# A fused linear-attention and feed-forward kernel: the feed-forward's hidden units renumbered, its first weight loaded by row chunks

## The chip, the cores and the metric

The kernel runs on one core of a Trainium2 chip. The metric is the device time of one execution in microseconds (us); the numbers given are medians of repeated runs. A core has five engines that run their own instruction streams: TensorE (PE; its weight loads are listed apart as PEld), VectorE (DVE), ScalarE (ACT), GpSimd (POOL) and SyncE (SP), which here issues the DMA transfers. An engine waits for another by a counting semaphore: GpSimd, for example, raises its count by one with each finished instruction, and a reader waits until the count stands at a given number.

## The reference

Inputs are q, k, v of 8 batches, 8 heads, 576 positions and 64 features in float32, and two weights: w_in (512 x 2048) and w_out (2048 x 512).

```python
def phi(x, c, s):
    r = np.maximum(x, 0.0)
    return np.concatenate([r * c, r * s], axis=-1)
q_p = phi(q, cos_w, sin_w)
k_p = phi(k, cos_w, sin_w)
kv = np.einsum('bhsf,bhsd->bhfd', k_p, v)
z = np.sum(k_p, axis=2)
num = np.einsum('bhsf,bhfd->bhsd', q_p, kv)
den = np.einsum('bhsf,bhf->bhs', q_p, z)[..., None] + 1e-06
attn_out = num / den
# tokens x 512, heads side by side
x = attn_out.transpose(0, 2, 1, 3).reshape(B * S, H * D)
h = x @ w_in
g = np.maximum(0.01 * h, h)
return g @ w_out
```

The order of the 2048 hidden units is free: the sum over them in the last product is the same if w_in's columns and w_out's rows are numbered in the same way.

## The kernel before

All matrix work is in fp16 with float32 sums. A batch's first 512 positions form one group of four tiles of 128 tokens (`MAIN`), and the last 64 positions of all eight batches form a ninth group, so the feed-forward runs over nine groups of 512 tokens (`g` = 0 to 8). For a group:

- `q_prep` (line 287) makes phi(q) on VectorE, `q_transpose` (312) turns it on PE through PSUM, and ScalarE copies it out. `k_main`, `k_tail`, `v_main`, `v_tail` (229 to 247) make phi(k) and v in fp16.
- `kv_half` (277) sums kv and z for four heads on PE and copies the sum out on ScalarE. `num` (321) multiplies one tile of queries by kv for all heads; `num_half` (353) does it for two tiles (a pair `jp`) and four heads (`hg`). `divide` (335) is three VectorE instructions behind either.
- `x_transpose` (386) turns one tile of attention output, `x_transpose_half` (368) a pair of tiles for four heads; ScalarE copies the result into `xT`, whose four row chunks of 128 are the 512 inputs of the feed-forward.
- `ffn1(g, m, lo, hi, chunks)` (396) computes one unit: 128 hidden units for token columns `lo` to `hi`, as one matmul for each row chunk, with a piece of `w1` as PE's weights. Two units share a PSUM tile `ps_h` of two banks, and one ScalarE Lrelu (412) takes the pair into `g`.
- `ffn2(g, i)` (416) computes one of four parts of a tile's output from four units of `g` and of `w2`; `ffn2_out` writes it.

The weights arrive in float32 in staging tiles and are cast to fp16 into `w1` and `w2`, both resident. The staging pool (`stage`, seven buffers, line 56) is shared with q, k and v. `load_w1` (128) loads columns `W1[i]` to `W1[i+1]` of w_in for all four row chunks: four pieces of 256 columns and two of 512. `load_w2` (134) loads 512 rows of w_out as four blocks of 128 rows, so that a partition takes four rows of 2 KB from four places. All loads go through SP's one queue.

The order of the instructions on each engine is that of the program text (`tc.manual_schedule()`); the framework adds the waits, from the regions that each instruction reads and writes. In the first batch (lines 480 to 529) the text is written out by hand: attention and ffn1 of group 0 are interleaved, ffn1 works on the first two tiles (`half` = 256 columns) as soon as these are there, then on the other two. `cast_w1` 0, 1 and 2 on GpSimd are recorded ahead of the first ffn1, 3 on VectorE further down (520), 4 and 5 after unit 7 (531 to 533). `idle(n)` issues n matmuls on a blank tile. From line 545 `weave` mixes units and steps by position numbers: group 0's remaining units, group 0's ffn2 with batch 1's attention, and then all other groups, in which ffn1 of the next group alternates with ffn2 of this one.

Of the kernel before, what the change touches and what calls it, by code (L numbers as in the profile page):

```python
# [9 lines left out]
dt = mybir.dt  # L10
AF = mybir.ActivationFunctionType
ALU = mybir.AluOpType

P = 128
J = 4
# [3 lines left out]
def kernel(  # L19
# [14 lines left out]
    nc = tc.nc  # L34
# [3 lines left out]
    DFF = moe_w_in.shape[1]  # L38
    MAIN = J * P
# [3 lines left out]
    NKC = DM // P  # L43
    NFT = DFF // P
# [5 lines left out]
    def pool(name, bufs, space=None):  # L50
        kw = {"space": space} if space is not None else {}
        return ctx.enter_context(tc.tile_pool(name=name, bufs=bufs, **kw))
# [3 lines left out]
    stage = pool("stage", 7)  # L56
# [11 lines left out]
    ps_h = pool("ps_h", 2, PS)  # L68
# [3 lines left out]
    def psum(where, shape, dtype, name):  # L72
        p = {"h": ps_h, "o": ps_o, "n": ps_n}[where]
        return p.tile(shape, dtype, name=name, tag="ps_" + where)

    st = {}
    ACT, DVE, POOL = nc.scalar, nc.vector, nc.gpsimd
# [42 lines left out]

    w1 = const.tile([P, NKC, DFF], dt.float16, name="w1")
    w2 = const.tile([P, NFT, DM], dt.float16, name="w2")

    W1 = [0, 256, 512, 768, 1024, 1536, 2048]
    w1v = moe_w_in.rearrange("(c p) f -> p c f", p=P)
    w2v = moe_w_out.rearrange("(m p) d -> p m d", p=P)

    def load_w1(i):
        lo, hi = W1[i], W1[i + 1]
        t = stage.tile([P, NKC, hi - lo], dt.float32, name="w1st", tag="stage")  # L130
        nc.sync.dma_start(t, w1v[:, :, lo:hi])
        st["w1", i] = t

    def load_w2(i):
        t = stage.tile([P, 4, DM], dt.float32, name="w2st", tag="stage")
        nc.sync.dma_start(t, w2v[:, 4 * i : 4 * i + 4, :])
        st["w2", i] = t

    load_main("q", q, 0, (0,))
# [1 line left out]
    load_kvtail("k", k, 0)  # L141
    load_kvtail("v", v, 0)
    load_halves(0)
    for i in range(4):
        load_w1(i)

# [3 lines left out]
    def idle(n):  # L152
        ps = psum("o", [P, MAIN], dt.float32, "ps_idle")
        for _ in range(n):
            nc.tensor.matmul(ps, lhsT=blank[:, 0:P], rhs=blank)  # L155
# [40 lines left out]
    for i in range(2):  # L196
# [5 lines left out]
        for o in range(2):  # L202
            sl = slice(o * TAIL, (o + 1) * TAIL)
# [15 lines left out]
    def copy(eng, o, i):  # L219
        if eng is ACT:  # L220
            nc.scalar.copy(o, i)  # L221
        else:
            eng.tensor_copy(o, i)  # L223
# [5 lines left out]
    def k_main(b, j, eng_c, eng_s, lo=0, hi=H):  # L229
        kpm, kst = st["kpm", b], st["k", b]  # L230
        for eng, t, f in ((eng_c, cos_t, 0), (eng_s, sin_t, D)):
            phi_half(
                eng, kpm[:, lo:hi, j, f : f + D], kst[:, lo:hi, j, :], t[:, j : j + 1]
            )
# [6 lines left out]
    def v_main(b, lo, hi, eng):  # L241
        copy(eng, vmain[b % 2][:, lo:hi, :, 0:D], st["v", b][:, lo:hi])
# [78 lines left out]
    def num(g, j, where="n"):  # L321
        qpT = st["qpT", g, j]
        ps = psum(where, [P, 2, 512], dt.float32, "ps_num")
        for b, lo, hi in q_src(g, j)[2]:
            for h in range(H):
                nc.tensor.matmul(  # L326
                    ps[lo:hi, h // 4, (h % 4) * NE : (h % 4 + 1) * NE],
                    lhsT=qpT[:, h, lo:hi],
                    rhs=kv[b][:, h, :],
                )  # L330
        xs = xspool.tile([P, H, D], dt.float16, name="xs")
        divide(ps, xs.rearrange("p (a b) e -> p a b e", a=2))
        st["xs", g, j] = xs
# [19 lines left out]
    def num_half(g, jp, hg, where):  # L353

        if hg == 0:
            st["xp", g, jp] = qppool.tile([P, 2, H, D], dt.float16, name="xp", tag="qp")
        ps = psum(where, [P, 2, 512], dt.float32, "ps_numh")
        for o in range(2):
            for hh in range(4):
                h = 4 * hg + hh  # L360
                nc.tensor.matmul(  # L361
                    ps[:, o, hh * NE : (hh + 1) * NE],
                    lhsT=st["qpT", g, 2 * jp + o][:, h, :],
                    rhs=kv[g][:, h, :],
                )
        divide(ps, st["xp", g, jp][:, :, 4 * hg : 4 * hg + 4, :])

    def x_transpose_half(g, jp, hg, ps=None, out=True):

        if ("xT", g) not in st:  # L370
            st["xT", g] = xtpool.tile([P, NKC, MAIN], dt.float16, name="xT")
        xp = st["xp", g, jp]
        if ps is None:
            ps = psum("o", [P, 2, 2 * P], dt.float16, "ps_xth")
        for cc in range(2):
            for o in range(2):
                h = 4 * hg + 2 * cc
                nc.tensor.transpose(
                    ps[:, cc, o * P : (o + 1) * P], xp[:, o, h : h + 2, :], ident
                )  # L380
        if out:
            nc.scalar.copy(  # L382
                st["xT", g][:, 2 * hg : 2 * hg + 2, jp * 2 * P : (jp + 1) * 2 * P], ps
            )

    def x_transpose(g, j, where="o"):
        xs = st["xs", g, j]
        ps = psum(where, [P, NKC, P], dt.float16, "ps_xt")
        for c in range(NKC):
            nc.tensor.transpose(ps[:, c, :], xs[:, 2 * c : 2 * c + 2, :], ident)  # L390
        nc.scalar.copy(xT_tile(g, j), ps)  # L391

    def ffn1(g, m, lo=0, hi=MAIN, chunks=range(NKC)):

        if ("g", g) not in st:
            st["g", g] = gpool.tile([P, NFT, MAIN], dt.float16, name="g")
        if m % 2 == 0 and chunks[0] == 0:
            st["h", m // 2] = psum("h", [P, 2, MAIN], dt.float32, "ps_h")  # L400
        xT = st["xT", g]
        ps = st["h", m // 2]
        for c in chunks:
            nc.tensor.matmul(  # L404
                ps[:, m % 2, lo:hi],
                lhsT=w1[:, c, m * P : (m + 1) * P],
                rhs=xT[:, c, lo:hi],
                start=(c == 0),
                stop=(c == NKC - 1),
            )  # L410
        if m % 2 == 1 and chunks[-1] == NKC - 1:
            nc.scalar.activation(  # L412
                st["g", g][:, m - 1 : m + 1, lo:hi], ps[:, :, lo:hi], AF.Lrelu
            )

    def ffn2(g, i, eng=DVE):
        tt, part = divmod(i, 4)
# [51 lines left out]
            queue = ACT if half and o else nc.sync  # L469
            queue.dma_start(out[r0 : r0 + TAIL, cols], osb[o * TAIL : (o + 1) * TAIL, :])  # L470

    def cast_w1(i, eng):
        copy(eng, w1[:, :, W1[i] : W1[i + 1]], st["w1", i])

    def cast_w2(i, eng):
        copy(eng, w2[:, 4 * i : 4 * i + 4, :], st["w2", i])
# [14 lines left out]
    for j in range(J):  # L491
        k_main(0, j, DVE, DVE, 0, 4)
    v_main(0, 0, 4, ACT)
    idle(6)
    kv_half(0, 0, "o")
    for j in range(J):
        k_main(0, j, ACT if j < 2 else DVE, DVE, 4, 8)
    v_main(0, 4, 6, DVE)
    v_main(0, 6, 8, ACT)
    idle(1)  # L500
    num_half(0, 0, 0, "n")
    idle(4)
    kv_half(0, 1, "o")
    for i in range(3):
        cast_w1(i, POOL)
    x_transpose_half(0, 0, 0)
    num_half(0, 0, 1, "h")
    num(0, 2, "n")
    half = 2 * P
    for m in range(2):  # L510
        ffn1(0, m, 0, half, range(0, 2))
    idle(1)
    x_transpose_half(0, 0, 1)
    for m in range(2, 4):
        ffn1(0, m, 0, half, range(0, 2))
    for m in range(2):
        ffn1(0, m, 0, half, range(2, 4))
    x_transpose(0, 2)
    num(0, 3, "n")
    cast_w1(3, DVE)  # L520
    for m in range(2, 4):
        ffn1(0, m, 0, half, range(2, 4))
    for m in range(4, 6):
        ffn1(0, m, 0, half)
    x_transpose(0, 3)
    for m in range(6, 8):
        ffn1(0, m, 0, half)
    for m in range(8):
        ffn1(0, m, half, MAIN)

    for i in range(4, 6):
        load_w1(i)
        cast_w1(i, POOL)
    load_w2(0)
    load_main("q", q, 1)
    load_kvtail("k", k, 1)
    load_kvtail("v", v, 1)
    for i in range(1, 4):
        load_w2(i)
    load_halves(1)  # L540
    load_main("q", q, 2)
# [3 lines left out]
    def weave(units, steps):  # L545

        steps = sorted(steps, key=lambda s: s[0])
        for at, u in units:
            while steps and steps[0][0] <= at:
                steps.pop(0)[1]()  # L550
            u()
        assert not steps

    def f1(g, m):
        return lambda: ffn1(g, m)
# [4 lines left out]
    steps = []  # L560

    def at(pos, f, *args):
        steps.append((pos, lambda: f(*args)))

    at(12, cast_w2, 0, DVE)
    weave([(m, f1(0, m)) for m in range(8, NFT)], steps)

    for j in range(J):  # L570
        q_prep(1, j)
    cast_w2(1, DVE)
    cast_w2(2, DVE)
    kp_tiles(1)
    k_tail(1, DVE, DVE)
# [2 lines left out]
    ps = psum("n", [P, 2, DM], dt.float32, "ps_o")  # L578
    for tt in range(2):
        st["ps_o", 0, 2 + tt] = ps[:, tt]  # L580
    steps = []
    for j in range(J):
        at(2 + j, q_transpose, 1, j, ACT, "h")
        at(9, k_main, 1, j, ACT, DVE, 0, 4)
    at(9, v_main, 1, 0, 2, DVE)
    at(9, v_main, 1, 2, 4, ACT)
# [19 lines left out]
    ps = psum("n", [P, 2, MAIN], dt.float16, "ps_x")  # L606
# [29 lines left out]
    steps = []  # L636
# [84 lines left out]
```

## Time and profile before

| What | Value |
|---|---|
| Median of 3 runs | 297.73 us (297.64 to 298.7) |
| The profiled execution | 297.93 us, of which the profiled span is 295.9 us |
| Instructions | 4849 |
| DMA | 56.93 MB, 91301 packets |
| L404 (ffn1) on PE | 608 matmuls, 143.0 us |
| L425 (ffn2) on PE | 560 matmuls, 139.3 us |
| L404 weight loads (PEld) | 608, mean 98 ns |
| L412 Lrelu on ACT | 76, mean 979 ns |
| L223 casts of w_in on POOL | 5, mean 1381 ns |

A row of the profile names a line of the kernel, the engine, the operation and the tiles (out <- in). In an order of time the first number is the start in us from the span's beginning, the second the time until the last of the merged instructions has ended; x is their number; the brackets tell how long the engine was idle before and what ended the wait. Matmuls overlap, so the mean time of one (368 ns for L404) is longer than the step from one to the next.

### The profile page before, as it was taken

The page shows a single profiled execution, that of the slowest core. Times are in us where ns is not written, and L with a number is a line of the kernel's source. Part 1 is how long each engine was busy: PE and PEld are TensorE (multiplying, and loading weights), DVE is VectorE, ACT ScalarE, POOL GpSimd, SP SyncE. Part 2 cuts the span into 40 slices and gives each one's busy share as a digit, 9 for nine tenths or more (in the row PEclk, how much of TensorE's full clock was granted, in tenths as well). Part 3 has the DMA queues.
Part 4 walks back from the last instruction along what each step waited for, and adds up shares of the span by engine and source line. Part 5 has one row for each costly group of instructions (what it writes and reads, how often), then busy time and mean ns, then how long its engine had stood idle before and what let it go on. Part 6 is the DMA issues. An engine that isn't in the chain of part 4 may idle for free.

```text
span 295.9 us, 4849 instructions
## 1 busy us (share of the span) xinstructions
PE 287.2 (97%) x1950; PEld 146.9 (50%) x1950; DVE 133.4 (45%) x329; ACT 108.2 (37%) x132; POOL 22.0 (7%) x33
## 2 busy tenths in 40 slices
PE   7889999999999999999999999999999999999994
PEld 3567556455455454454445444544444444444444
DVE  5950668934754927723861356233323211000011
ACT  4855546665163422242223222322222232222200
POOL 2045000000000400200400040000000000000000
PEclk9999999999999999999999999999999999999999
DMA  7999999999999999989659985716671211011132
GB/s 215 348 366 372 322 366 347 325 154 325 258 257 290 203 293 264 226 196 302 178 124 230 315 148 125 110 53 144 139 162 55 71 53 38 35 47 60 38 71 71
DMA packets 91301, 56.93 MB, mean 192 GB/s; under 512 B 56848, under 2 KB 83728, under 8 KB 91280
## 3 DMA queue, kind: packets, MB, share of 16 engines
q1 hardware_dynamic: 91200, 56.57, 74.1%
q8 instruction: 15, 0.25, 0.4%
q10 hardware_dynamic: 80, 0.07, 0.1%
q14 instruction: 6, 0.05, 0.0%
HBM read 36.70 MB, written 9.44 MB: 156 GB/s over the span
## 4 chain that ended last, share of the span: by engine, by line
PE 81%; DMA 11%; ACT 3%; SPq 2%; DVE 1%; issue 0%; POOL 0%
PE ps_h L404 37%; PE ps_o L425 36%; DMA qst<-in_q_dram 7%; DMA vst<-in_v_dram 3%; PE ps_num L326 3%; SPq L86 2%; PE ps_kv L263 2%; ACT qpT L221 1%; DMA out_dram<-osb 1%; PE ps_kvh L263 1%; ACT xT L382 1%; PE ps_kv L253 0%; PE ps_numh L361 0%; ACT g L412 0%; ACT xT L609 0%
## 5 line engine op out<-in xcount | busy, mean ns | idle before, releaser
L404 PE MATMUL ps_h<-xT,w 128*128 128x512 f16 (+1 forms) x608 | 143.0, 368 | 1.4 <-ACT xT L391 0.8
L425 PE MATMUL ps_o<-w,g 128*128 128x512 f16 x560 | 139.3, 379 | 0.0
L412 ACT ACTIVATE g<-ps_h 128x1024 f16<-128x1024 f32 (+1 forms) x76 | 74.3, 979 | 143.3 <-PE ps_h L404 143.2
L404 PEld LDWEIGHTS <-w 128*128 128x128 f16 x608 | 57.0, 98 | 60.0 <-issue 1.6
L425 PEld LDWEIGHTS <-g 128*128 128x128 f16 x560 | 54.1, 98 | 63.0
L223 DVE COPY osb<-ps_o 128x512 f32<-128x512 f32 x33 | 22.7, 691 | 81.1 <-PE ps_o L425 80.9
L337 DVE TENSOR_SCALAR den<-ps_num 128x8 f32<-128x8 f32 x30 | 5.0, 166 | 53.9 <-PE ps_num L326 53.9
L342 DVE TENSOR_TENSOR xs<-ps_num,rden 128x512 f16<-128x512 f32 x30 | 20.7, 691 | 1.0
L223 POOL CAST vmain<-vst 128x1024 f16<-128x1024 f32 (+1 forms) x9 | 9.7, 1096 | 134.4 <-DMA vst<-in_v_dram 86.3
L215 DVE TENSOR_SCALAR qp<-qst,cos_t 128x512 f16<-128x512 f32 (+1 forms) x34 | 16.6, 488 | 4.0 <-DMA qst<-in_q_dram 4.0
L215 DVE TENSOR_SCALAR kpm<-kst,sin_t 128x512 f16<-128x512 f32 (+1 forms) x40 | 18.0, 466 | 0.3 <-DMA kst<-in_k_dram 0.3
L215 DVE TENSOR_SCALAR qp<-qst,sin_t 128x512 f16<-128x512 f32 (+1 forms) x34 | 16.0, 469 | 0.0
L326 PEld LDWEIGHTS <-qpT 128*128 128x128 f16 (+1 forms) x272 | 11.9, 101 | 7.4 <-issue 1.7
L215 DVE TENSOR_SCALAR kpm<-kst,cos_t 128x512 f16<-128x512 f32 (+1 forms) x29 | 13.9, 480 | 0.1
L326 PE MATMUL ps_num<-kv,qpT 128*128 128x66 f16 (+1 forms) x272 | 13.3, 194 | 0.0
L263 PEld LDWEIGHTS <-kpm 128*128 128x128 f16 x256 | 10.6, 97 | 2.4 <-DVE kpm L215 0.7
L155 PE MATMUL ps_idle<-blank 128*128 128x512 f16 x30 | 9.7, 457 | 1.2 <-DVE blank L150 1.2
L221 ACT COPY qpT<-ps_qt 128x1024 f16<-128x1024 f16 x8 | 7.8, 1019 | 4.7 <-PE ps_qt L316 4.7
L223 DVE CAST w<-w2st 128x2048 f16<-128x2048 f32 x4 | 4.9, 1227 | 10.0 <-DMA w2st<-in_moe_w_out_dram 10.0
L223 POOL CAST w<-w1st 128x1024 f16<-128x1024 f32 (+1 forms) x5 | 6.9, 1381 | 19.1 <-DMA w1st<-in_moe_w_in_dram 19.1
L263 PE MATMUL ps_kv<-vmain,kpm 128*128 128x66 f16 x192 | 8.1, 193 | 0.0
L341 DVE RECIPROCAL rden<-den 128x8 f32<-128x8 f32 x36 | 7.3, 203 | 1.2
(58 smaller groups left out, 100.0 us busy)
## 6 DMA issues: line engine op xcount, KB each, us to landing
out_dram<-osb SPq DMA_DIRECT2D x32, 256.0 KB, 2.8
qst<-in_q_dram SPq DMA_DIRECT2D x7, 1024.0 KB, 6.6
kst<-in_k_dram SPq DMA_DIRECT2D x6, 1024.0 KB, 7.6
vst<-in_v_dram SPq DMA_DIRECT2D x6, 1024.0 KB, 7.9
w2st<-in_moe_w_out_dram SPq DMA_DIRECT2D x4, 1024.0 KB, 10.2
kst<-in_k_dram SPq DMA_DIRECT2D x4, 512.0 KB, 8.6
vst<-in_v_dram SPq DMA_DIRECT2D x4, 512.0 KB, 8.4
w1st<-in_moe_w_in_dram SPq DMA_DIRECT2D x4, 512.0 KB, 9.2
```

What stands on the lines that cost most here:

```text
L86: nc.sync.dma_start(st[nm, b][:, lo:hi], src[b, lo:hi, 0:MAIN, :].rearrange("h (p j) d -> p h j d", j=J),)
L155: nc.tensor.matmul(ps, lhsT=blank[:, 0:P], rhs=blank)
L215: eng.tensor_scalar(out=o, in0=i, scalar1=0.0, scalar2=col, op0=ALU.max, op1=ALU.mult)
L221: nc.scalar.copy(o, i)
L223: eng.tensor_copy(o, i)
L263: nc.tensor.matmul(ps[:, (2 * cc + o) * NE : (2 * cc + o + 1) * NE], lhsT=kpm[:, h, j, :], rhs=vmain[b % 2][:, h, j, :], start=False, stop ...
L326: nc.tensor.matmul(ps[lo:hi, h // 4, (h % 4) * NE : (h % 4 + 1) * NE], lhsT=qpT[:, h, lo:hi], rhs=kv[b][:, h, :],)
L341: nc.vector.reciprocal(rden, den)
L342: nc.vector.tensor_tensor(out=xs, in0=ps[:, :, 0 : 4 * NE].rearrange("p a (b e) -> p a b e", e=NE)[:, :, :, 0:D], in1=rden.rearrange("p (a ...
L404: nc.tensor.matmul(ps[:, m % 2, lo:hi], lhsT=w1[:, c, m * P : (m + 1) * P], rhs=xT[:, c, lo:hi], start=(c == 0), stop=(c == NKC - 1),)
L412: nc.scalar.activation(st["g", g][:, m - 1 : m + 1, lo:hi], ps[:, :, lo:hi], AF.Lrelu)
L425: nc.tensor.matmul(ps, lhsT=st["g", g][:, m, tt * P : (tt + 1) * P], rhs=w2[:, m, :], start=(m == 0), stop=(m == NFT - 1),)
```

## The change

The hidden units get a new numbering. In block i (512 units) unit 4i + r now holds w_in's columns 512i + 4p + r for p = 0 to 127, and w_out's rows of the same numbers. A partition of `w2` thus takes four consecutive rows, 8 KB, and PE reads its ffn1 weights out of `w1` at every fourth column. w_in is loaded in eight pieces, (block, row-chunk pair), each of 128 partitions x 2 chunks x 512 columns, all issued at the start; eight casts on GpSimd, recorded ahead of the first ffn1, take their place. In the first batch both pairs of tiles now go through `num_half` and `x_transpose_half`; ffn1's units 0 to 3 run over both halves, chunks 0 and 1 first, then 2 and 3; units 4 to 15 run over 512 columns, the first two in the PSUM tile "n". Two of `k_main`'s calls move ahead of `kv_half(0, 0)`. w_out's second piece is loaded ahead of batch 1's q, its cast moves to position 14, and batch 1's four `q_transpose` move three positions back.

```diff
-    W1 = [0, 256, 512, 768, 1024, 1536, 2048]
+    NB = DFF // 512
     w1v = moe_w_in.rearrange("(c p) f -> p c f", p=P)
-    w2v = moe_w_out.rearrange("(m p) d -> p m d", p=P)
+    w1m = w1.rearrange("q c (i p r) -> q c i r p", p=P, r=4)
+    w2v = moe_w_out.rearrange("(i p r) d -> i p r d", p=P, r=4)
...
+    def load_w1(i, cp):
+        if cp == 0:
+            st["w1", i] = stage.tile([P, NKC, 512], dt.float32, name="w1st", tag="stage")
+        sl = slice(2 * cp, 2 * cp + 2)
+        nc.sync.dma_start(st["w1", i][:, sl], w1v[:, sl, 512 * i : 512 * (i + 1)])
...
-        nc.sync.dma_start(t, w2v[:, 4 * i : 4 * i + 4, :])
+        nc.sync.dma_start(t, w2v[i])
...
-    for i in range(4):
-        load_w1(i)
+    for i in range(NB):
+        for cp in range(2):
+            load_w1(i, cp)
...
-                lhsT=w1[:, c, m * P : (m + 1) * P],
+                lhsT=w1m[:, c, m // 4, m % 4, :],
                 rhs=xT[:, c, lo:hi],
-                start=(c == 0),
-                stop=(c == NKC - 1),
+                start=(c == 0 and lo == 0),
+                stop=(c == NKC - 1 and hi == MAIN),
...
-    def cast_w1(i, eng):
-        copy(eng, w1[:, :, W1[i] : W1[i + 1]], st["w1", i])
+    def cast_w1(i, cp, eng):
+        sl = slice(2 * cp, 2 * cp + 2)
+        copy(eng, w1[:, sl, 512 * i : 512 * (i + 1)], st["w1", i][:, sl])
...
+    for j in range(2):
+        k_main(0, j, ACT, DVE, 4, 8)
     idle(6)
     kv_half(0, 0, "o")
-    for j in range(J):
-        k_main(0, j, ACT if j < 2 else DVE, DVE, 4, 8)
+    for j in range(2, J):
+        k_main(0, j, DVE, DVE, 4, 8)
...
     num_half(0, 0, 0, "n")
-    idle(4)
+    num_half(0, 1, 0, "h")
+    idle(3)
     kv_half(0, 1, "o")
-    for i in range(3):
-        cast_w1(i, POOL)
+    for i in range(NB):
+        for cp in range(2):
+            cast_w1(i, cp, POOL)
     x_transpose_half(0, 0, 0)
-    num_half(0, 0, 1, "h")
-    num(0, 2, "n")
+    num_half(0, 0, 1, "n")
     half = 2 * P
     for m in range(2):
         ffn1(0, m, 0, half, range(0, 2))
-    idle(1)
-    x_transpose_half(0, 0, 1)
+    x_transpose_half(0, 1, 0)
     for m in range(2, 4):
         ffn1(0, m, 0, half, range(0, 2))
...
+    num_half(0, 1, 1, "n")
+    x_transpose_half(0, 0, 1)
+    for m in range(4):
+        ffn1(0, m, half, MAIN, range(0, 2))
+    x_transpose_half(0, 1, 1)
+    for m in range(4):
         ffn1(0, m, 0, half, range(2, 4))
...
+    for m in range(4):
+        ffn1(0, m, half, MAIN, range(2, 4))
...
-    for i in range(4, 6):
-        load_w1(i)
-        cast_w1(i, POOL)
-    load_w2(0)
+    for i in range(2):
+        load_w2(i)
...
+    for m in range(4, 6):
+        ffn1(0, m, where="n")
     at(12, cast_w2, 0, DVE)
-    weave([(m, f1(0, m)) for m in range(8, NFT)], steps)
+    at(14, cast_w2, 1, DVE)
+    weave([(m, f1(0, m)) for m in range(6, NFT)], steps)
```

## The prediction

> **What bounds the kernel now.** I read the table by stage first, then TensorE's (PE's) order of time, then who waited. The stage rows give, after the stretch, its length, busy time of PE, PEld, DVE, ACT, POOL, the granted clock, the DMA share and GB/s.
>
> ```profile
> PE 287.2 (97%) x1950; PEld 146.9 (50%) x1950; DVE 133.4 (45%) x329; ACT 108.2 (37%) x132; POOL 22.0 (7%) x33
> ...
> 15.50:22.20 6.70, 5.45 (x67) 4.01 (x66) 3.78 (x10) 4.17 (x8) 3.04 (x3) 1.00 1.08 368
> 22.20:33.50 11.30, 11.30 (x73) 7.07 (x74) 1.78 (x3) 6.06 (x8) 3.79 (x2) 1.00 1.09 341
> 33.50:62.00 28.50, 27.73 (x219) 15.03 (x218) 23.38 (x58) 18.22 (x27) 0.61 (x1) 1.00 1.12 330
> 62.00:284.00 222.00, 222.00 (x1440) 108.97 (x1438) 90.32 (x211) 69.75 (x75) 12.47 (x16) 1.00 0.68 161
> 292.20:295.30 3.10, 0.00 (x0) 0.00 (x0) 0.00 (x0) 0.33 (x1) 0.00 (x0) 1.00 0.28 71
> 295.40:295.80 0.40, 0.00 (x0) 0.00 (x0) 0.00 (x0) 0.00 (x0) 0.00 (x0) 0.50 0.00 0
> ```
>
> From 22.2 us on PE is busy in every microsecond but some 0.8, all of them before 62. Whatever delays PE in the first 35 us therefore reaches the end undiminished, and whatever brings it forward reaches the end only until the next input is late. The DMA engines are saturated to 62 us (330 to 368 GB/s). The last two rows matter below: PE's last matmul ends at 292.1, and the clock is 1.00 until 295.3, then 0.50.
>
> ```profile
> 1.19 5.16 PE L155 MATMUL ps_idle<-blank 128*128 128x512 f16 x14 [1.19 <-DVE blank L150]
> 15.43 1.04 POOL L223 CAST w<-w1st 128x1024 f16<-128x1024 f32 x1 [12.63 <-DMA w1st<-in_moe_w_in_dram]
> 16.55 0.60 PE L404 MATMUL ps_h<-xT,w 128*128 128x256 f16 x4
> 16.93 1.04 POOL L223 CAST w<-w1st 128x1024 f16<-128x1024 f32 x1 [0.47 <-DMA w1st<-in_moe_w_in_dram]
> 18.55 1.04 POOL L223 CAST w<-w1st 128x1024 f16<-128x1024 f32 x1 [0.58 <-DMA w1st<-in_moe_w_in_dram]
> 21.44 0.69 DVE L223 CAST w<-w1st 128x1024 f16<-128x1024 f32 x1 [0.51 <-DMA w1st<-in_moe_w_in_dram]
> 22.20 11.45 PE L404 MATMUL ps_h<-xT,w 128*128 128x256 f16 x72 [0.80 <-ACT xT L391]
> 24.18 1.89 POOL L223 CAST w<-w1st 128x2048 f16<-128x2048 f32 x1 [4.60 <-DMA w1st<-in_moe_w_in_dram]
> 26.89 1.89 POOL L223 CAST w<-w1st 128x2048 f16<-128x2048 f32 x1 [0.82 <-DMA w1st<-in_moe_w_in_dram]
> 33.48 1.89 PE L425 MATMUL ps_o<-w,g 128*128 128x512 f16 x8
> 48.98 0.57 PE L263 MATMUL ps_kvh<-vmain,kpm 128*128 128x66 f16 x8 [0.21 <-POOL vmain L223]
> ```
>
> Each cast starts as its piece of w_in lands. With 1 KB packets 0.5 MB takes 1.50 to 1.62 us (15.43, 16.93, 18.55); with 2 KB packets 1 MB takes 2.71 (24.18 to 26.89), so 1.36 per 0.5 MB. PE's paces: a 512-column matmul 216 ns (four in 0.86 in the chain of waits); a 256-column one 109 (the 72 of 22.20 end their issue at 33.48, 11.28 us later; less 32 x 0.216 leaves 4.37 for 40); a transpose 56 (eight from 35.20 to 35.65); a 66-column one 32 (16 from 47.19 to 47.70).
>
> **The change, part by part.**
>
> *The waits on w_in's casts: the term that decides.* In the changed program, as built, PE's first ffn1 weight load (unit 0, row chunk 0) waits for GpSimd's count 8, its first cast. The second (unit 0, chunk 1) waits for count 14, which only the seventh cast raises: block 3, chunks 0 and 1. The third wait, at chunk 3, is for count 15, the eighth and last cast; after that no ffn1 load waits on GpSimd at all. The data needed is only the first cast's, but the eight casts are all recorded ahead of ffn1, and a cast over two chunks is treated as touching the other blocks' reads in chunks 1 and 3. The old program waits for counts 8, 9 and 10, one DVE cast, then 11 and 12, each just ahead of the units that use it.
>
> When does the seventh cast end? The first 0.5 MB landed for the cast at 15.43; at 2 KB packets it comes 0.15 earlier, 15.28. Six more steps of 1.36 give 23.44; the cast is still 128x1024, 1.04 us, shorter than a step, so none queues: it ends at 24.5. PE reaches that load at about 16.8: attention of the first half, 16.0 to 16.5 as now, then one matmul. The 0.1 that ScalarE's two k pieces add ahead of its kv copy (0.91 us of ACT, in the gap from 12.3 to 13.2) lies far ahead of this. So PE stands for 7.7 us. Behind that load in PE's order stands everything: transposes, the fourth num_half, all of ffn1 and ffn2; ScalarE's Lrelu and VectorE's last divide wait for it. One lateness in the old stream is the bound above: the fourth piece came 2.89 after the third instead of 1.5, 1.4 us late. The packet records show a 16 KB instruction packet of 1.13 us at 17.91, when PE had begun 272 instructions. The changed PE stops at its 251st, before that fetch; I take 0.1 and keep 0 to 1.4. PE resumes at 24.6.
>
> *What is left for PE then.* 31 matmuls of 256 columns (units 0 to 3 in halves, one done) 3.38, 48 of 512 (units 4 to 15) 10.37, 12 transposes 0.67, 8 of 66 columns 0.25: 14.7 us, to ffn2's start at 39.3, against 33.48 now. Of latencies, the last pair's divide (0.17 + 0.20 + 0.69 and hand-overs, 1.2 us behind its num) beside 0.22 + 0.87 of PE work leaves about 0.2. Warm, ffn2 starts at 39.5, 6.0 late.
>
> *The clock.* PE stands 7.8 us. The start of the trace shows PE at half pace: the warm-up matmuls' weight loads follow each other by 0.43 us, twice 0.216, until about 5.2, 4.0 us after the first; its end shows 0.50 some 3.2 us after the last matmul. So PE resumes at half pace, and I take 4.0 us of it: half of that, 2.0, is lost, less the 0.2 of latency that it covers. Bounds: 0, if a pause in the middle is treated otherwise than the end, and 3 us, if the clock takes half as long again. Sum: ffn2 at 41.3, 7.8 late.
>
> [...]
>
> *Read with a step of four.* All 576 ffn1 weight loads of nine groups now read fp16 at every fourth place, 8 bytes apart. No load in the trace does that. Contiguous ones take 98 ns, and follow each other every 32 ns under the 66-column matmuls, each of which has its own load. If each fetched column cost four times as much, 4 x 32 = 128 ns still hides under 216; 32 matmuls of 256 columns would pay 19 ns each, 0.6 us. Bounds 0 to 0.6; I take 0, since the half-pace part covers most of it. It would need over 216 ns, seven times the row, to cost anything in the 544 others.
>
> [...]
>
> *Packets and order of loads.* w_in's 2 MB that had 1 KB packets gains 4 x 0.15 = 0.6 us of queue time. w_out in 8 KB packets gains, by 1 to 2 KB, 0 to 0.3 us per MB more. SP issues two extra w_in loads, and w_out's second piece ahead of q of batch 1; no buffer wait stands before w_in's eight (seven buffers, four for w_in). All of it is hidden: w_out is wanted after 41 and comes by about 29 to 32, its third and fourth pieces by about 42 against a use after 49, and VectorE's casts (1.23 each) stand in that slack. The last v of batch 1 lands near 47 while PE gets there at 56, so the wait at 48.98 goes: 0.3 saved. If PE were not late, this wait would be the bound.
>
> *The rest.* Pairs of tiles in place of single ones are the same columns on PE and the same four divides on VectorE; two idle matmuls fewer, and eight Lrelus of 512 columns that become four of 1024, lie beside the stall.
>
> **Sum**, on the profiled execution (297.93 us, span 295.9, 2.0 around it): + 6.0 + 2.0 - 0.2 - 0.3 = + 7.5, so 305.4. The median of the runs is 0.2 lower, which I leave inside the rounding.
>
> **Rivals.**
> 1. *The clock holds full.* All as above without 2.0: about 303.6. Against: half pace at the start, 0.50 at the end.
> 2. *The stream is late too, or the clock returns late.* 1.4 more before the seventh cast, or up to 1 to 1.5 more at half pace: about 306.8. For: the 2.89 step; against: PE's place at that fetch.
> 3. *Strided weight loads bind.* At 250 ns each, 34 ns x 544 = 18 us more: 323. It decides from 216 ns. Against: the room of seven times.
> 4. *Not slower: the long wait does not hold PE.* If PE took each block as its casts land (1.36 per half block), ffn1 would end near 30 and PE would meet batch 1's v, which lands 1.2 to 1.5 earlier than now: 296.5. It decides from a seventh cast that ends before 18; the DMA rows put it at 24.5, since 3.5 MB must land first. That the program doesn't do what it says is this case too.
>
> **How the numbers follow.** Forecast 0.72, rival 1 0.09, rival 2 0.11, rival 3 0.04, rival 4 0.04. The range 303.3 to 307.2 takes in rivals 1 and most of 2. A measurement here tells 0.5% (1.5 us) from nothing; only rival 4 lies on that side: faster 0.03, same 0.02, slower 0.95.
>
> **What would show it.** PE idle from about 16.8 to 24.6, ended by GpSimd's cast; after it 256-column matmuls at about 0.21 us for some 4 us, then 0.109; ffn2's first matmul near 41.3; no PE wait on v in batch 1; ffn1 weight loads' mean under 216 and 512-column matmuls at 216 from 62 us on. I am wrong if PE passes chunk 1 at 17, if the pace after the pause is full, or if the steady stage is longer than 222 us for the same matmuls.

## The result and the profile after

The changed kernel takes 306.15 us (median of 5 runs, 305.79 to 307.04) against 297.67 before: a ratio of 1.0283, 95% interval 1.0268 to 1.0299. The forecast was 305.4 in 303.3 to 307.2. The profiled execution is the longest of the five, 307.04 us with a span of 304.9, so its parts add up to 9.0 us of span where the medians differ by 8.5.

PE's order of time in the changed kernel, start and length in us, waits in brackets:

```profile
15.90 0.42 PE L365 MATMUL ps_numh<-kv,qpT 128*128 128x66 f16 x8 [0.19 <-ACT kv L284]
16.39 0.27 PE L408 MATMUL ps_h<-xT,w 128*128 128x256 f16 x1
25.66 0.83 PE L408 MATMUL ps_h<-xT,w 128*128 128x256 f16 x3 [9.00 <-POOL w L227]
...
28.43 1.91 PE L408 MATMUL ps_h<-xT,w 128*128 128x256 f16 x8
...
30.56 12.61 PE L408 MATMUL ps_h<-xT,w 128*128 128x256 f16 x64
43.01 4.48 PE L427 MATMUL ps_o<-w,g 128*128 128x512 f16 x20
...
58.07 0.42 PE L267 MATMUL ps_kvh<-vmain,kpm 128*128 128x66 f16 x8
```

One matmul of the first unit runs, then PE stands for 9.00 us until a cast on GpSimd. What follows starts late: ffn2 at 43.01 where it was 33.48, 9.5 later. That this is close to the length of the pause is chance: the slow clock after the pause adds to it (below), and the new order, which without the pause is quicker to ffn2, takes from it. At 58.07, where the kernel before waited for batch 1's v, there is no wait now; PE comes after the data. GpSimd's order of time tells which cast it was:

```profile
15.10 1.04 POOL L227 CAST w<-w1st 128x1024 f16<-128x1024 f32 x1 [12.31 <-DMA w1st<-in_moe_w_in_dram]
16.45 1.04 POOL L227 CAST w<-w1st 128x1024 f16<-128x1024 f32 x1 [0.31 <-DMA w1st<-in_moe_w_in_dram]
17.80 1.04 POOL L227 CAST w<-w1st 128x1024 f16<-128x1024 f32 x1 [0.32 <-DMA w1st<-in_moe_w_in_dram]
20.50 1.04 POOL L227 CAST w<-w1st 128x1024 f16<-128x1024 f32 x1 [1.66 <-DMA w1st<-in_moe_w_in_dram]
...
24.56 1.04 POOL L227 CAST w<-w1st 128x1024 f16<-128x1024 f32 x1 [0.31 <-DMA w1st<-in_moe_w_in_dram]
25.91 1.04 POOL L227 CAST w<-w1st 128x1024 f16<-128x1024 f32 x1 [0.30 <-DMA w1st<-in_moe_w_in_dram]
```

The seventh cast ends at 25.60 and PE goes on at 25.66, with the eighth not yet begun. Each cast waits for its DMA, one piece every 1.35 us, except that the fourth came after 2.70. The stage table (after the length: busy time of PE, PEld, DVE, ACT, POOL, then the clock) shows what the pause did to PE:

```profile
16.70:20.90 4.20, 0.00 (x0) 0.00 (x0) 0.75 (x2) 0.00 (x0) 2.23 (x3) 1.00 1.06 385
21.10:25.60 4.50, 0.00 (x0) 0.00 (x0) 0.00 (x0) 0.00 (x0) 3.56 (x4) 0.50 1.06 411
25.70:31.20 5.50, 5.50 (x38) 4.32 (x39) 2.51 (x5) 1.57 (x3) 1.04 (x1) 0.50 1.03 380
31.30:36.00 4.70, 4.70 (x30) 3.16 (x29) 2.23 (x5) 3.05 (x4) 0.00 (x0) 1.00 1.13 300
...
71.00:293.00 222.00, 222.00 (x1439) 115.99 (x1437) 90.28 (x211) 69.69 (x75) 12.10 (x16) 1.00 0.66 158
```

The clock is halved at 21.0, 4.3 us after PE's last matmul, and comes back at 31.2, 5.6 us after PE has resumed. The steady stage is as before: 222.0 us for 1439 matmuls. The groups by form show the weight loads (PEld) of ffn1, line 408, read at every fourth place, beside those of ffn2, line 427, without gaps:

```profile
L408 PEld LDWEIGHTS <-w 128*128 128x128 f16 x592 | 65.0, 115 | 63.4 <-POOL w L227 9.4 <-issue 1.4
L427 PEld LDWEIGHTS <-g 128*128 128x128 f16 x560 | 54.1, 98 | 61.5
```

A load's mean went from 98 to 115 ns; the matmuls that cover it take 216.

### The profile page after: what moved, and what is told of

The parts are those of the page before. It is cut to its first block, busy times and chain, and to the rows that moved or that the text cites. A ratio compares the mean times of both kernels' runs of the same rounds, so it can differ in the third digit from the quotient of the medians.

```text
span 304.9 us, 4811 instructions
## 1 busy us (share of the span) xinstructions
PE 288.1 (94%) x1932; PEld 155.4 (51%) x1932; DVE 132.5 (43%) x328; ACT 107.5 (35%) x128; POOL 23.1 (8%) x36
## 4 chain that ended last, share of the span: by engine, by line
PE 88%; DMA 7%; SPq 2%; ACT 1%; POOL 0%; issue 0%; DVE 0%
PE ps_h L408 41%; PE ps_o L427 39%; DMA w1st<-in_moe_w_in_dram 4%; PE ps_num L330 3%; DMA kst<-in_k_dram 2%; PE ps_kv L267 2%; SPq L96 1%; DMA out_dram<-osb 1%; SPq L86 1%; PE ps_qt L320 1%; PE ps_xth L382 0%; PE ps_numh L365 0%; PE ps_kv L257 0%; ACT xT L386 0%; POOL w L227 0%; ACT g L416 0%
## 5 line engine op out<-in xcount | busy, mean ns | idle before, releaser
L408 PE MATMUL ps_h<-xT,w 128*128 128x512 f16 (+1 forms) x592 | 145.1, 378 | 9.6 <-POOL w L227 9.0
L416 ACT ACTIVATE g<-ps_h 128x1024 f16<-128x1024 f32 x72 | 73.4, 1023 | 141.9 <-PE ps_h L408 141.8
L408 PEld LDWEIGHTS <-w 128*128 128x128 f16 x592 | 65.0, 115 | 63.4 <-POOL w L227 9.4
L346 DVE TENSOR_TENSOR xs<-ps_num,rden 128x512 f16<-128x512 f32 x28 | 19.4, 691 | 1.0
L219 DVE TENSOR_SCALAR kpm<-kst,sin_t 128x512 f16<-128x512 f32 (+1 forms) x40 | 16.7, 433 | 0.3 <-DMA kst<-in_k_dram 0.3
L330 PEld LDWEIGHTS <-qpT 128*128 128x128 f16 (+1 forms) x256 | 11.2, 101 | 7.3 <-issue 1.7
L330 PE MATMUL ps_num<-kv,qpT 128*128 128x66 f16 (+1 forms) x256 | 12.4, 194 | 0.0
L267 PEld LDWEIGHTS <-kpm 128*128 128x128 f16 x256 | 10.4, 97 | 2.0 <-DVE kpm L219 0.7
L159 PE MATMUL ps_idle<-blank 128*128 128x512 f16 x28 | 8.5, 437 | 1.2 <-DVE blank L154 1.2
L227 POOL CAST w<-w1st 128x1024 f16<-128x1024 f32 x8 | 8.3, 1040 | 15.8 <-DMA w1st<-in_moe_w_in_dram 15.8
L386 ACT COPY xT<-ps_xth 128x512 f16<-128x512 f16 x6 | 3.4, 587 | 14.1 <-PE ps_xth L382 14.1
```

The lines of the kernel that those rows point to most:

```text
L219: eng.tensor_scalar(out=o, in0=i, scalar1=0.0, scalar2=col, op0=ALU.max, op1=ALU.mult)
L267: nc.tensor.matmul(ps[:, (2 * cc + o) * NE : (2 * cc + o + 1) * NE], lhsT=kpm[:, h, j, :], rhs=vmain[b % 2][:, h, j, :], start=False, stop ...
L330: nc.tensor.matmul(ps[lo:hi, h // 4, (h % 4) * NE : (h % 4 + 1) * NE], lhsT=qpT[:, h, lo:hi], rhs=kv[b][:, h, :],)
L346: nc.vector.tensor_tensor(out=xs, in0=ps[:, :, 0 : 4 * NE].rearrange("p a (b e) -> p a b e", e=NE)[:, :, :, 0:D], in1=rden.rearrange("p (a ...
L408: nc.tensor.matmul(ps[:, m % 2, lo:hi], lhsT=w1m[:, c, m // 4, m % 4, :], rhs=xT[:, c, lo:hi], start=(c == 0 and lo == 0), stop=(c == NKC ...
L416: nc.scalar.activation(st["g", g][:, m - 1 : m + 1, :], ps, AF.Lrelu)
```

## The experiments

**Eight tiles in place of one.** The regions of different casts can't be confused when each has its own tile.

```diff
-    w1 = const.tile([P, NKC, DFF], dt.float16, name="w1")
+    w1 = [const.tile([P, 2, 512], dt.float16, name=f"w1_{n}") for n in range(DFF // 256)]
...
-                lhsT=w1m[:, c, m // 4, m % 4, :],
+                lhsT=w1m[2 * (m // 4) + c // 2][:, c % 2, m % 4, :],
...
-        copy(eng, w1[:, sl, 512 * i : 512 * (i + 1)], st["w1", i][:, sl])
+        copy(eng, w1[2 * i + cp], st["w1", i][:, sl])
```

> w1 as eight separate fp16 tiles, one for each cast, everything else as in the changed kernel. Theory (the long wait comes from ffn1's second weight load being held until the seventh cast, and all else in the change is harmless): PE's loads wait for casts 1, 2, 3 ... one by one, ffn2 of group 0 starts at 30 to 31.5 us instead of 43.0, and PE then meets batch 1's v, which lands near 46.9: kv of the second four heads starts near 47.6 instead of 48.98 in the kernel before, total 296.0 to 297.0. Rival (weight loads read with a step of four, or the new order itself, cost the time): 301 us or more, PE still late at ffn2.

Measured: 296.86 us (295.91 to 298.94, 10 runs), ratio to before 0.9977, interval 0.9957 to 0.9997. PE's order of time:

```profile
16.23 0.60 PE L410 MATMUL ps_h<-xT,w 128*128 128x256 f16 x4
...
19.27 12.27 PE L410 MATMUL ps_h<-xT,w 128*128 128x256 f16 x64
31.37 4.48 PE L429 MATMUL ps_o<-w,g 128*128 128x512 f16 x20
...
46.84 0.57 PE L269 MATMUL ps_kvh<-vmain,kpm 128*128 128x66 f16 x8 [0.25 <-POOL vmain L229]
```

The four matmuls at 16.23 go through, no cast is waited for, and ffn2 starts at 31.37, 11.6 sooner than in the changed kernel and, by these two profiles, 2.1 sooner than in the one before; the profiled execution here is the fastest of the ten (295.91 us). With everything else of the change in place, 9.3 us of 306.15 are gone: the wait, with the slow clock after it, was the whole loss. The wait at 46.84 is the one for batch 1's v, back as the next bound, 0.8 sooner than expected.

**The pause filled with blank matmuls.** The wait stays; the clock should not fall.

```diff
     num_half(0, 0, 1, "n")
+    idle(38)
```

> The changed kernel with 38 matmuls on the blank tile put ahead of the first ffn1 matmul (38 x 0.216 = 8.2 us from 16.5); the long wait stays, the clock need not fall. Theory (part of the loss is PE's half pace after the pause, 5.6 us of it in the changed kernel's profile, so 2.8): ffn2 starts near 40.5 instead of 43.0, total 303.3 to 304.0. Rival (the pace after the pause costs nothing because latencies of VectorE and ScalarE bound that stretch anyway): 305.5 to 306.3.

Measured: 304.12 us (303.98 to 304.53, 4 runs), just above the 303.3 to 304.0 expected and well under the rival's 305.5. In the stage table the clock is 1.00 before, in and after the rest of the pause; below it stand two rows of PE's order of time:

```profile
16.00:24.00 8.00, 8.00 (x43) 3.64 (x40) 1.18 (x4) 0.16 (x1) 5.20 (x5) 1.00 1.07 394
24.50:25.20 0.70, 0.00 (x0) 0.00 (x0) 0.00 (x0) 0.00 (x0) 0.70 (x1) 1.00 0.99 410
25.30:29.00 3.70, 3.57 (x43) 3.29 (x44) 2.10 (x4) 1.76 (x3) 1.04 (x1) 1.00 0.98 397
```

```profile
25.26 0.52 PE L408 MATMUL ps_h<-xT,w 128*128 128x256 f16 x3 [0.80 <-POOL w L227]
...
40.26 4.48 PE L427 MATMUL ps_o<-w,g 128*128 128x512 f16 x20
```

So 2.0 us of the loss, by the medians, is PE's half pace after the pause; the other 7.3 (304.12 less the 296.86 of eight tiles) are the waiting itself. ffn2 started at 40.26; of the 2.75 us that this is sooner than 43.01, 0.4 come from a pause that ended at 25.26, since w_in landed a little sooner in this execution. In the profiles the half pace thus cost 2.35 us.

**The old numbering with all else of the change.** One w1 tile, the same eight casts over two chunks, contiguous weight reads, w_out in 2 KB packets.

```diff
-    w1m = w1.rearrange("q c (i p r) -> q c i r p", p=P, r=4)
-    w2v = moe_w_out.rearrange("(i p r) d -> i p r d", p=P, r=4)
+    w1m = w1.rearrange("q c (i r p) -> q c i r p", p=P, r=4)
+    w2v = moe_w_out.rearrange("(i r p) d -> i p r d", p=P, r=4)
```

> The old numbering of the units (contiguous weight reads, w_out in 2 KB packets) with all else of the change, one w1 tile and the same eight casts of two chunks. Theory (it is the step of four in the read that makes the wait too wide; the same casts with contiguous reads are waited for one by one): ffn2 starts at 30 to 31.5, batch 1's v lands some 0.8 us later than with 8 KB packets, total 296.7 to 297.7. Rival (the casts over two chunks make the wait wide, as the prediction's wording had it): the pause stays, 305 to 306.5.

Measured: 296.68 us (295.99 to 297.72, 10 runs), ratio 0.9964, interval 0.9951 to 0.9978. ffn2 starts at 31.72, and the weight loads are back at their old mean. PE's order of time, then the group of loads by form:

```profile
16.57 0.60 PE L408 MATMUL ps_h<-xT,w 128*128 128x256 f16 x4
...
31.72 4.48 PE L427 MATMUL ps_o<-w,g 128*128 128x512 f16 x20
```

```profile
L408 PEld LDWEIGHTS <-w 128*128 128x128 f16 x592 | 55.7, 98 | 60.2 <-issue 1.5 <-DVE xp L346 0.2
```

The casts are those of the changed kernel, and PE's built waits now are for counts 8, 9, 10 and so on. So the cast over two chunks alone does not make the wait wide; the read with a step of four is needed. The read alone does not do it either: in the changed program the load of chunk 0, which has the same step, waits only for its own cast, and the changed program with one cast for each row chunk, built but not timed, waits for its casts one by one although the reads keep their step. It takes the two together. (A comparison of first and last addresses would give just this, since a cast of block 3 over chunks 0 and 1 reaches from the end of chunk 0 through all of chunk 1. How the framework compares regions is not shown here.)

**A second series, with a control.** In the seven kernels that follow, the 52 transposes by DMA of groups 2 to 8 are done on PE, so all are longer; they are compared with each other, and nothing before 50 us is touched.

```diff
-            at(start + j * step + lag, q_transpose_dma, b, j)
+            at(start + j * step + lag, q_transpose, b, j, ACT, "h")
-            at(start + j * step + lag, x_transpose_dma, b, j)
+            at(start + j * step + lag, x_transpose, b, j, "h")
```

> The changed kernel with batch 2 to 8's 52 transposes by DMA done on PE instead (copied out by ScalarE): the control for the three runs beside it. It can touch only what comes after 50 us. Both theories: the pause from 16.5 to about 25.6 and ffn2's start near 43.0 are as in the changed kernel; 28 x 8 + 24 x 4 transposes at 56 ns add 17.9 us of PE work, total about 324, more if PE waits for the copies.

Measured: 331.54 us (331.29 to 331.95, 4 runs), more than the 324 expected, for the most part since PE now also waits for ScalarE's copies (some 6 us of waits for ScalarE after 50 us, 0.6 in the changed kernel). The pause is there, 16.7 to 25.31, but ffn2 starts at 41.51, 1.5 us sooner than in the changed kernel's profile:

```profile
25.31 0.83 PE L396 MATMUL ps_h<-xT,w 128*128 128x256 f16 x3 [8.59 <-POOL w L227]
...
41.51 4.48 PE L415 MATMUL ps_o<-w,g 128*128 128x512 f16 x20
```

The stage table tells why:

```profile
18.40:25.30 6.90, 0.00 (x0) 0.00 (x0) 0.00 (x0) 0.00 (x0) 4.73 (x5) 0.50 1.06 400
25.30:28.50 3.20, 3.19 (x25) 2.62 (x26) 0.54 (x3) 0.76 (x2) 1.04 (x1) 0.50 0.99 406
28.60:35.00 6.40, 6.40 (x45) 4.58 (x44) 3.62 (x6) 4.05 (x6) 0.00 (x0) 1.00 1.14 309
```

Here the clock fell between 18.2 and 18.4, was 0.50 to 28.5 and came back 3.2 us after PE resumed, not 5.6. The half clock lasted about as long in both, 10.24 us in the changed kernel (21.00 to 31.24 in its clock records) and 10.1 to 10.4 by these rows; it began at different times.

**PE stopped 20 instructions earlier.**

```diff
-    idle(6)
     kv_half(0, 0, "o")
...
-    idle(1)
     num_half(0, 0, 0, "n")
     num_half(0, 1, 0, "h")
-    idle(3)
```

> That control without ten of its blank matmuls (the groups of 6, 1 and 3 around the first kv), so that PE stands in its long wait 20 instructions earlier in its program. Theory (the fourth piece of w_in came 1.35 us late in the changed kernel because PE's next 16 KB of instructions were fetched at 17.2 us through one of the same DMA engines, and the fetch is asked for by PE's place in its program): it now comes after the pause, the pieces of w_in land every 1.35 us without a gap, the seventh cast ends near 24.2 instead of 25.6, total 1.0 to 1.6 us under the control's. Rival (the late piece belongs to the stream, whatever PE does): the gap stays, total within 0.4 of the control's.

Measured: 331.60 us (331.27 to 332.81, 4 runs), no different from the control. GpSimd's casts:

```profile
17.74 1.04 POOL L227 CAST w<-w1st 128x1024 f16<-128x1024 f32 x1 [0.32 <-DMA w1st<-in_moe_w_in_dram]
19.57 1.04 POOL L227 CAST w<-w1st 128x1024 f16<-128x1024 f32 x1 [0.78 <-DMA w1st<-in_moe_w_in_dram]
21.25 1.04 POOL L227 CAST w<-w1st 128x1024 f16<-128x1024 f32 x1 [0.64 <-DMA w1st<-in_moe_w_in_dram]
```

The theory fell: in the packet records the 16 KB instruction packet still comes in the pause, at 17.92, with PE 20 instructions short of where it stood in the changed kernel. The stream still loses 0.8 us around it, 0.48 and 0.33 of the two steps after 17.74. In the kernel before and in the changed one, too, the long step is the one in which this packet ends (17.91 to 19.04 and 17.22 to 18.32 in the packet records; the casts around it start at 18.55 and 21.44, and at 17.80 and 20.50), with 1.4 and 1.35 us lost. That the packet causes the gap is thus likely; a run without it was not made. The run is no clean test of the total either: without the blank matmuls the clock fell to 0.50 at 12.7, ahead of the pause.

**Columns put in order by the casts.**

```diff
-        copy(eng, w1[:, sl, 512 * i : 512 * (i + 1)], st["w1", i][:, sl])
+        for c in range(2 * cp, 2 * cp + 2):
+            copy(
+                eng,
+                w1[:, c, 512 * i : 512 * (i + 1)].rearrange("q (r p) -> q r p", p=P),
+                st["w1", i][:, c].rearrange("q (p r) -> q r p", r=4),
+            )
...
-                lhsT=w1m[:, c, m // 4, m % 4, :],
+                lhsT=w1[:, c, m * P : (m + 1) * P],
```

> That control with the new numbering and its 8 KB packets kept, but GpSimd's casts put the columns in the units' order (two casts of 128x512 for each piece, each reading at every fourth place and writing without gaps), so PE's weight loads are contiguous again; one w1 tile. Theory (only the strided read makes the wait wide): waits are one by one, ffn1 weight loads' mean is back at 98 ns from 115, ffn2 starts at 31 to 32 as with eight tiles if two casts take at most the 1.36 us of a piece's landing, total 8.5 to 10 us under the control's. Rival (the permuting casts are slower than the landing, over 0.68 each): PE waits for casts in units 4 to 15, ffn2 starts after 32.5.

Measured: 324.50 us (324.23 to 324.76, 4 runs), 7.0 under the control. GpSimd's group, then PE's order of time:

```profile
L226 POOL CAST w<-w1st 128x512 f16<-128x512 f32 x16 | 16.7, 1110 | 12.6 <-DMA w1st<-in_moe_w_in_dram 12.6
```

```profile
23.84 3.63 PE L395 MATMUL ps_h<-xT,w 128*128 128x512 f16 x16 [0.64 <-POOL w L226]
28.01 3.63 PE L395 MATMUL ps_h<-xT,w 128*128 128x512 f16 x16 [0.55 <-POOL w L226]
32.18 2.98 PE L395 MATMUL ps_h<-xT,w 128*128 128x512 f16 x13 [0.55 <-POOL w L226]
35.00 4.48 PE L414 MATMUL ps_o<-w,g 128*128 128x512 f16 x20
```

Contiguous reads again go with narrow waits (each cast here also covers one chunk only). But a cast that gathers every fourth float32 takes as long for 512 elements (16.7 us for 16) as the plain one for 1024, 2.1 us for a piece that lands every 1.35; GpSimd becomes the bound and ffn2 starts at 35.0: the rival's case.

**A step of sixteen.**

```diff
-    w1m = w1.rearrange("q c (i p r) -> q c i r p", p=P, r=4)
-    w2v = moe_w_out.rearrange("(i p r) d -> i p r d", p=P, r=4)
+    w1m = w1.rearrange("q c (p r) -> q c r p", r=NFT)
+    w2v = moe_w_out.rearrange("(p i r) d -> i p r d", p=P, r=4)
...
-                lhsT=w1m[:, c, m // 4, m % 4, :],
+                lhsT=w1m[:, c, m, :],
```

> That control with the units numbered over the whole width: unit m takes columns 16p + m, so weight loads read at every sixteenth place, 32 bytes apart; w_out still in 8 KB packets. The long wait is the same. Theory (a weight load has 216 ns beside a 512-column matmul, and the step of four cost 17 ns of it, so the step is hidden): loads' mean between 115 and 200 ns, 512-column matmuls still 216 ns apart, total within 0.5 of the control's. Rival (a longer step costs in proportion to the distance and comes over 216): 512-column ffn1 matmuls further apart than 216 ns, total 3 us or more over the control's.

Measured: 332.01 us (331.86 to 332.44, 4 runs), 0.5 over the control. PE's first ffn1 matmul, then the loads of ffn1:

```profile
25.09 1.07 PE L396 MATMUL ps_h<-xT,w 128*128 128x256 f16 x4 [8.66 <-POOL w L227]
```

```profile
L396 PEld LDWEIGHTS <-w 128*128 128x128 f16 x592 | 80.6, 146 | 48.1 <-POOL w L227 8.8 <-issue 3.6
```

The long wait is a true one here: a unit takes columns of all four blocks, so that even the first load needs the seventh cast. A load takes 146 ns, where the control has 114 and contiguous ones 98. This hides under 216 for the most part, but no longer wholly: the 560 ffn1 matmuls of 512 columns have 140.6 us of busy time, against 139.6 in the control, and the profiled span is 1.0 us longer (330.2 against 329.2) after the same start of ffn2 (41.50 and 41.51).

**The change without its wait, against the kernel before, in the second series.** Eight tiles, the kernel before, and the old numbering, each with the later transposes on PE.

> Eight w1 tiles (the new numbering, strided reads, w_out in 8 KB packets) with the transposes of batches 2 to 8 on PE, as in the control. Theory (the long wait is all that is wrong with the change): ffn2 starts near 31.4 instead of 41.5, total 9.5 to 10.5 us under the control's 331.5, so 321.0 to 322.0. Rival (something else in the change costs time later on): above 323.

> The kernel before with the transposes of batches 2 to 8 on PE: what the change without its wait is to be compared with. Theory (the change without its wait reaches ffn2 2.1 us sooner, 31.37 against 33.48, and keeps it): 1.5 to 2.5 us above the run with eight tiles, 322.8 to 324.2. Rival (it is given back to a later wait on batch 1's inputs): within 1.0 of it.

> The old numbering (contiguous reads, w_out in 2 KB packets) with all else of the change, transposes of batches 2 to 8 on PE. Theory (8 KB packets bring batch 1's v 1.2 us sooner, and PE waits for it): 0.7 to 1.4 us above the run with eight tiles. Rival (the strided reads cost as much as the packets bring, or neither counts): within 0.4 of it.

Measured: eight tiles 322.58 us (322.19 to 322.81), the kernel before 323.43 (323.24 to 323.61), the old numbering 322.54 (322.12 to 323.11), 4 runs each. So the change without its wait is worth 0.85 us, less than the 1.5 to 2.5 expected and inside the rival's 1.0, and eight tiles are 9.0 us under the control, not 9.5 to 10.5. The start of ffn2 in the kernel before, then PE's order of time with eight tiles:

```profile
32.75 1.89 PE L413 MATMUL ps_o<-w,g 128*128 128x512 f16 x8
```

```profile
31.65 4.48 PE L417 MATMUL ps_o<-w,g 128*128 128x512 f16 x20
...
42.41 1.89 PE L417 MATMUL ps_o<-w,g 128*128 128x512 f16 x8 [0.18 <-DVE w L229]
44.61 0.41 PE L269 MATMUL ps_kvh<-vmain,kpm 128*128 128x66 f16 x8 [0.26 <-DVE vmain L229]
47.84 0.57 PE L269 MATMUL ps_kvh<-vmain,kpm 128*128 128x66 f16 x8 [0.21 <-POOL vmain L229]
```

The lead at ffn2 is 1.1 us, not the 2.1 that the expectation took from two single profiles: the kernel before is 0.7 sooner there than in its first profile (33.48), as the fourth piece of its w_in came 0.7 sooner (its cast starts at 20.71, in the first profile at 21.44). With eight tiles PE is early and waits for w_out's last cast and twice for batch 1's v: the rest of the difference is given back there. Between the two numberings there is no difference, here or in the first pair (296.86 and 296.68), though the profiles of that pair have the last of these waits end at 46.84 and 48.06. What 8 KB packets bring in these runs can't be told from the scatter of the landings.

## Why the prediction was right

- **The long wait for the seventh cast: right**, in its place (PE stands at the second weight load), in its releaser and in being, with the slow clock behind it, the whole loss. Its reason was half of it: the prediction put the wait down to a cast over two chunks; the old numbering with the same casts has narrow waits, so the read with a step of four is needed as well.
- **The end of that cast: the term that was mis-sized.** "PE resumes at 24.6" was 25.66. The stream began 0.18 sooner than I had it and lost 1.35 at the fourth piece. I had taken 0.1 for that and kept up to 1.4, on my estimate that PE's place in its program brings the instruction packet; the packet came at 17.22 all the same, and in the second series it came with PE 20 instructions earlier still.
- **The half pace: right, too small for the profiled execution.** I took 4.0 us of it, costing 2.0. The profile has 5.6 us: from the pause's end to ffn2 PE took 17.35 us, and 15.00 with the filled pause, so it cost 2.35. In the control it lasted 3.2 us and cost 1.2 (25.31 to 41.51 is 16.20). The median cost, from the filled pause, is 2.0. The half clock itself was about as long in both, 10.24 us and 10.1 to 10.4; it began 4.7 us before the pause's end in the changed kernel (21.00 to 25.66) and some 7.0 before it in the control, and so more of it was left behind the pause in the first. It does not always last as long: in the run without blank matmuls it was 17.0 to 17.2 us (12.6 or 12.7 to 29.7 or 29.8). The second rival's 1 to 1.5 us more at half pace is shown by no run; 0.35 more is the most that was (2.35 for 2.0). The clock fell 1.6 us after PE's last matmul in the control (16.72 to about 18.3) and 4.3 after it in the changed kernel (16.66 to 21.00).
- **Work left after the pause: right.** At full clock it was to take 14.9 us (14.7 and 0.2 of latency); with the filled pause it took 15.00. Forecast 41.3 for ffn2, plus 1.06 for the later end and 0.55 for the dearer half pace (2.35 for 2.0 - 0.2) is 42.9; measured 43.01.
- **Strided loads cost nothing: right.** They grew by 17 ns, from 98 to 115, beside matmuls 216 ns apart, and 296.86 us with them (eight tiles) stands beside 296.68 with contiguous ones. The prediction's counts are off: there are 592 of these loads, not 576, and 560 of them, not 544, beside 512-column matmuls. As their cost was put at 0, the sum does not change.
- **The wait for v goes: right.** 9.53 us at ffn2 became 9.0 at the end; 0.3 was forecast, about 0.5 came.
- **Packets.** w_out's third and fourth megabyte are 2.51 us apart (casts at 38.42 and 40.93) against 2.74 before (39.53 and 42.27), inside the bound of 0 to 0.3, and hidden as said.
- **The rival without the wait was well priced:** 296.5 forecast, 296.86 and 296.68 measured, with batch 1's inputs as the next bound.

On the profiled execution the sum was + 7.5. Missing were 1.06 of pause, 0.55 of half pace and 0.1 of work, and 0.2 more was saved, which makes + 9.0; the span grew by 9.0. The medians, + 8.5, lie between.

## What to carry to other kernels

After a change of layout, read the semaphore values that the first readers wait for, and compare them with the last writer of the data they need: here reads with a step of four, over casts of two row chunks, turned "the first cast" into "the seventh of eight". Where reads are strided, give each separately written piece its own tile (296.86 us here, 306.15 without). On PE, which is busy to the end here, the pause cost 7.3 us of waiting and 2.0 of slow clock after it; and of a lead of 1.1 us at ffn2, 0.85 was left at the end, as much as PE's last wait for batch 1's v ended sooner (47.84 against 48.69).

## What was not expected of the hardware

- A weight load of 128 x 128 fp16 takes 98 ns contiguous, 115 with a step of 4 places and 146 with a step of 16; beside matmuls 216 ns apart the first two cost no time that showed, the third 0.5 us of 332 by the medians and 1.0 in the profiles.
- An instruction packet of 16 KB (1.13 and 1.10 us in the packet records) started at 17.91 us in the kernel before and at 17.22 in the changed one, at 17.92 with PE stopped 20 instructions earlier, and w_in in flight came 1.4, 1.35 and 0.8 us late, over one piece or two. That the one causes the other is likely and not shown.
- The clock fell in the control after PE had stood for only 1.6 us, in the changed kernel after 4.3; it was then halved for 10.1 to 10.4 and for 10.24 us, and for 17.0 to 17.2 in the run without blank matmuls.
- On GpSimd a cast of 128 x 512 that reads every fourth float32 takes about as long (16.7 us for 16) as a plain one of 128 x 1024 (1.04).
